# Two dense stages of a three-part kernel re-tiled from superblocks of 768 tokens to superblocks of 1024 and one of 512

## The chip, the cores and the metric

The kernel runs on one core of a Trainium2 chip. The metric is the time of one execution on the device in microseconds (us). Before the change it was 1660.44 us, the median of three runs (1659.65 to 1664.32).

## The reference

Attention within chunks of 64 tokens (8 batches, 8 heads, 576 tokens, head size 64), then two dense layers on the 4608 tokens that come out, in float32:

```python
scores = scale * q_c @ k_c.T                    # within chunks of 64
out = softmax(scores) @ v_c                     # -> x, 4608 x 512
h = x @ w_in                                    # first layer, 512 -> 2048
g = np.where(h > 0.0, h, np.exp(np.minimum(h, 0.0)) - 1.0)
x = g @ w_out                                   # second layer, 2048 -> 512
gate = 1.0 / (1.0 + np.exp(-(x @ w_gate)))      # 512 -> 1536
val = x @ w_val                                 # 512 -> 1536
return gate * val @ w_out2                      # last product, 1536 -> 512
```

## The kernel before

Every operand of a dense product is split into a high and a low part of type float32r, and each product of two operands is three matmuls (high by high, low by high, high by low: `PASSES`). From the second layer on, the matrices are also multiplied in seven products of half-size blocks in place of eight (Strassen's way, in Winograd's form): sums and differences of blocks are formed on VectorE, split, multiplied, and the seven results added up from the four pairs of PSUM banks `bank_x`, `bank_w`, `bank_y`, `bank_z` in the order `PRODUCTS`.

There are four stages, one after the other on TensorE.

- **First layer with attention** (`stage_1`, L367): blocks of 512 tokens, matmuls of 512 columns at L393. Its result goes to DRAM as `gd`, in nine blocks. At its end `one` finishes the last block.
- **Second layer** (`stage_2`, L668): superblocks of 2 x `NL` = 768 tokens, so six of them, matmuls of `NL` = 384 columns at L710. For each superblock there are seven products `i` with four parts `p` (`QM`), 12 matmuls per part. Beside each part, `beside` puts the work for the parts to come: `load_b` fetches raw blocks from `gd`, `sub_b` forms block differences, `split_b` splits for product `i + 1`. `after` adds a product up and stores to `ymid`.
- **Gate and value** (`unit`, L840): the same superblocks. `load_x`, `sum_x`, `split_x` prepare the seven inputs `xc` of a superblock; then six units `q` (`QU`), of seven products with 12 matmuls each at L849, in the order `seq`, which runs forwards and backwards by turns. Each unit evicts into two tiles `s` and `t`, takes sigmoids on ScalarE, and a `finish`, called in the next unit, multiplies gate by value on VectorE and stores to `gvd`.
- **Last product** (`product` in `stages_3_4`, L982): nine groups of 512 tokens, seven products of 36 matmuls of 256 columns.

All order is written out by hand: an engine does its instructions in program order, and a tile's slot is waited for where its last reader is not done. Two pools matter. The pool `w` has `NW` = 28 slots of 4 KB. It holds weights, the tiles of the weight conversion that goes on in the background (`convert_pairs`, stepped by `bg`), and small tiles by `four`. The pools `six_right` and `six_left` have 10 and 4 slots of 6 KB, handed out by `get` in the order in which they were freed; they hold raw blocks, splits (`gc`, `xc`), and `s` and `t`.

Weights come from DRAM in tiles of 512 KB (`wd`), issued on POOL's queue at L335. `hold(at, room, ahead)` looks at the list of all uses from position `at` on, drops what is used no more, and loads the next `ahead` different ones, as far as they have been converted; when more than `room` are held, the one whose next use is farthest goes. `room(...)` is 28 less its arguments. In the second layer `ahead` is 10, in gate and value 14, in its last three units 22:

```python
need = list(soon)[:min(ahead, room)]
...
while len(held) >= room:
    del held[max(held, key=soon.get)]
```

Loads of raw blocks and all stores of results go through SP's queue.

Of the kernel before, what the change touches and what calls it, by code (L numbers as in the profile page):

```python
# [36 lines left out]
EARLY = 2  # L37
SLACK = 4
# [8 lines left out]
NL = 384  # L47
NJ = NT // (2 * NL)
ML = NL // 128
# [9 lines left out]
def kernel(  # L59
# [14 lines left out]
    ymid = [dram.tile([128, 2, 2, 2, NL], F32, name=f"ymid{j}") for j in range(NJ)]  # L74
    gvd = [dram.tile([128, 4, QU, NL], F32, name=f"gv{j}") for j in range(NJ)]
# [263 lines left out]
    six, idle, owner = {}, [], {}  # L339

    def open_sixes(side, n):
        six[side] = ctx.enter_context(tc.tile_pool(name=f"six_{side}", bufs=n, side=side, reuse_waits="tile"))
        idle.extend([side] * n)
# [8 lines left out]
    right_first = []  # L352

    def get(key, shape, dtype=F32):
        p = idle.pop(idle.index("right") if right_first and "right" in idle else 0)
# [8 lines left out]
    def four(*shape):  # L364
        return shaped(w_p.tile([128, 1024], F32, tag="w", name="four"), shape)
# [275 lines left out]
    def load_x(j, h):  # L641
        t = xt[j, h] = get("x", (2, 2, NL))
        for k in range(2):
            nc.sync.dma_start(out=t[:, k], in_=ymid[j][:, h, k])

    def sum_x(j, i):
        lo, hi = xt[j, 0], xt[j, 1]
        if i == 1:
            t = xt[j, 2] = get("x", (2, 2, NL))
            nc.vector.tensor_sub(out=t[:, 0], in0=hi[:, 0], in1=lo[:, 0])  # L650
        elif i == 2:
            t = xt[j, 2]
            nc.vector.tensor_sub(out=t[:, 1], in0=hi[:, 1], in1=t[:, 0])
        elif i == 3:
            nc.vector.tensor_sub(out=hi[:, 0], in0=hi[:, 1], in1=hi[:, 0])
        elif i == 4:
            nc.vector.tensor_sub(out=lo[:, 1], in0=lo[:, 1], in1=xt[j, 2][:, 1])

    def split_x(j, i):
        n, k = ((0, 0), (2, 1), (2, 0), (1, 0), (0, 1), (1, 1), (0, 1))[i]  # L660
        t = xc[j, i] = get("xc", (2, 2, NL), F32R)
        split(xt[j, n][:, k], t[:, 0], t[:, 1], nc.scalar, nc.vector)
# [5 lines left out]
    def stage_2(one):  # L668
# [5 lines left out]
        def load_b(j, k):  # L674
            if j >= NJ:
                return
            par, h = KEYS[k]
            for s in range(2):
                t = raw[j, k, s] = get(k, (HF // 2, NL))
                at, end, o = (2 * j + h) * NL, (2 * j + h + 1) * NL, 0  # L680
                while at < end:
                    blk, c = divmod(at, TB)
                    n = min(TB - c, end - at)
                    nc.sync.dma_start(
                        out=t[:, :, o:o + n], in_=gd[blk][:, par, 4 * s:4 * s + 4, c:c + n],
                    )
                    at, o = at + n, o + n

        def sub_b(j, out, a, b, s):
            if j >= NJ:  # L690
                return
            if (j, out, s) not in raw:
                raw[j, out, s] = get(out, (HF // 2, NL))
            nc.vector.tensor_sub(out=raw[j, out, s], in0=raw[j, a, s], in1=raw[j, b, s])

        def split_b(j, i, p):
            if j >= NJ:
                return
            src = raw[j, FROM[i], p // 2][:, 2 * (p % 2):2 * (p % 2) + 2]
            t = gc[j, i, p] = get("gc", (2, 2, NL), F32R)  # L700
            split(src, t[:, 0], t[:, 1], nc.scalar, nc.vector)
            if i in (2, 3, 5, 6) and p % 2 == 1:
                free(raw.pop((j, FROM[i], p // 2)))

        def product(j, i, p):
            t, w = gc.pop((j, i, p)), held["mid", p, i]
            for k in range(2):
                for u in range(2):
                    for n, (zw, zx) in enumerate(PASSES):
                        nc.tensor.matmul(  # L710
                            out=bank[PRODUCTS[i]][:, u, 0:NL],
                            lhsT=w[:, k, zw, 128 * u:128 * u + 128],
                            rhs=t[:, zx, k],
# [4 lines left out]
            free(t)  # L718

        def after(j, i):  # L720
            ps = bank[PRODUCTS[i]][:, :, 0:NL]

            def new(k):
                three[k] = three_p.tile([128, 2, NL], F32, tag="three", name=k)
                return three[k]
# [23 lines left out]
        def beside(j, i, p):  # L749

            nxt, h, odd = j + 1, p // 2, p % 2 == 1
# [49 lines left out]
        open_sixes("right", 10)  # L801
        end = NB * HF
        for n in range(HF):
# [7 lines left out]
            hold(0, room(F1 - 2 * n - 2), SLACK + 1 + n)  # L811
        for j in range(NJ):
            for i in range(7):
                for p in range(QM):
                    product(j, i, p)
                    if j == i == p == 0:
                        one(end, False)
                        pa.close()
                        right_first.append(True)
                        open_sixes("left", 4)  # L820
# [3 lines left out]
                    beside(j, i, p)  # L824
                    if j == NJ - 1:
                        for f in first_x.get((i, p), ()):
                            f()
                    if (j, i, p) == (1, 0, 0):
                        hold(7 * QM, room(8), 10)
                        convert_pairs(range(PAIRS_1, PAIRS_2), nc.gpsimd)  # L830
                    if i in (2, 3, 5) and p > 0 and j > 0:
# [8 lines left out]
    def unit(n):  # L840
        j, q = seq[n]
        last, third = n % QU == QU - 1, n % QU == QU - 3
        for i, c in enumerate(PRODUCTS):
            ps = bank[c][:, :, 0:NL]
            w = held["glu", q, i]
            for b in range(2):
                for k in range(2):
                    for p, (zw, zx) in enumerate(PASSES):
# [3 lines left out]
                            rhs=xc[j, i][:, zx, k],  # L852
# [4 lines left out]
            if last:  # L857
                free(xc.pop((j, i)))
            hold(MID + 7 * n + i + 1, room(9 if todo else 0), 14 if n < len(seq) - 3 else 22)
            if i == 0:  # L860
                s, t = get("s", (2, 2, NL)), get("t", (2, 2, NL))
# [39 lines left out]
        def finish():  # L901
            nc.vector.tensor_tensor(out=s[:, :, 0], in0=s[:, :, 1], in1=s[:, :, 0], op=ALU.mult)
            nc.sync.dma_start(out=gvd[j][:, 0:2, q], in_=s[:, :, 0])
            nc.vector.tensor_tensor(out=c12[:, 0], in0=c12[:, 1], in1=c12[:, 0], op=ALU.mult)
# [5 lines left out]
    def stages_3_4():  # L910

        G = NT // 512
# [3 lines left out]
        def load_g(g, c):  # L916
            if g >= G:
                return
            t = cs[g, c] = get(c, (QU, 256))
            for k in range(2):  # L920
                j, m = divmod(2 * g + k, ML)
                nc.sync.dma_start(
                    out=t[:, :, 128 * k:128 * k + 128], in_=gvd[j][:, C[c], :, 128 * m:128 * m + 128],
                )
        def split_g(g, i, c, keep=False):
            src = cs[g, c] if keep else cs.pop((g, c))
            gc[g, i] = []
            for h in range(2):
                t = get("gc", (2, QU // 2, 256), F32R)
                split(src[:, 3 * h:3 * h + 3], t[:, 0], t[:, 1], nc.scalar, nc.vector)  # L930
                gc[g, i].append(t)
# [41 lines left out]
        def product(g, i):  # L973
# [4 lines left out]
            for q in range(QU):  # L978
                t, w = tiles[q // 3], held["out2", q // 2, i]
                for p, (zw, zx) in enumerate(PASSES):  # L980
                    for m in range(2):
                        nc.tensor.matmul(  # L982
                            out=po[c][:, m],
                            lhsT=t[:, zx, q % 3, 128 * m:128 * m + 128],
# [5 lines left out]
            for t in tiles:  # L990
                free(t)

        def after(g, i):
# [6 lines left out]
            def store(h):  # L1000
                for n in range(2):
                    j, m = divmod(2 * g + n, ML)
                    r = (2 * j + h) * NL + 128 * m
# [29 lines left out]
        for n in range(N):  # L1033
            if n == 2:
                hold(MID + 7 * n, room(9), 14)
# [74 lines left out]
```

## Time and profile before

| | |
|---|---|
| median of three runs | 1660.44 us |
| profiled execution | 1665.95 us |
| its span | 1664.2 us |
| TensorE busy | 1630.8 us (98%), 11484 matmuls |
| VectorE busy | 1204.4 us (72%) |
| ScalarE busy | 742.9 us (45%) |
| GpSimd busy | 248.9 us (15%) |
| DMA | 387.76 MB, mean 233 GB/s |

The span runs from the first to the last instruction of the profiled execution. Busy times are sums over the whole span; the stages differ, so they are read stage by stage. Matmuls are pipelined: the duration shown for a single one is longer than the distance from one to the next, so the price of a matmul is taken from the length of a run of them. In the rows PE is TensorE, PEld its weight loads, DVE is VectorE, ACT is ScalarE, POOL is GpSimd and SP is the engine that issues most loads and stores; L710 is line 710 of the kernel.

### The profile page before, as it was taken

To read this page: it belongs to the slowest core of one execution; us is meant where nothing else is said; L and a number is where in the kernel's file an instruction comes from. 1 tells how busy PE (TensorE), PEld (TensorE's weight loads), DVE (VectorE), ACT (ScalarE), POOL (GpSimd) and SP (SyncE) were. 2 spreads that over 40 slices of the span, in tenths; PEclk is the share of its full clock that TensorE was granted. 3 is DMA by queue.
4 is the path that set the end of the run, shared out by engine and by line. 5 is a ranking of instruction groups with operands and counts; after the bars stand their busy time and mean duration, and the time that the engine had idled before them with its cause. 6 is when DMAs were issued, how large, how long until landed. Compare 5 with 4: busy or idle time off the path is not lost.

```text
span 1664.2 us, 28660 instructions
## 1 busy us (share of the span) xinstructions
PE 1630.8 (98%) x11484; PEld 1526.8 (92%) x11484; DVE 1204.4 (72%) x1653; ACT 742.9 (45%) x1184; POOL 248.9 (15%) x413
## 2 busy tenths in 40 slices
PE   6899999999999999999999999999999999999998
PEld 4677777777789999999999999999999999999998
DVE  7778888888636799876865677765555647777776
ACT  5666667667544454434432433322221313334343
POOL 3332111222210021100121021313010120000000
PEclk9999999999999999999999999999999999999999
DMA  6668888899897589944788397787472696463641
GB/s 225 196 213 292 293 294 280 285 294 295 283 353 262 203 287 305 313 152 149 253 252 288 108 315 267 266 310 276 173 247 82 204 354 189 138 167 112 167 128 51
DMA packets 231445, 387.76 MB, mean 233 GB/s; under 512 B 14352, under 2 KB 134160, under 8 KB 230288
## 3 DMA queue, kind: packets, MB, share of 16 engines
q1 hardware_dynamic: 169344, 203.46, 37.8%
q0 software_dynamic: 61968, 182.48, 33.0%
q8 instruction: 90, 1.47, 0.4%
q14 instruction: 43, 0.35, 0.1%
HBM read 253.23 MB, written 132.64 MB: 232 GB/s over the span
## 4 chain that ended last, share of the span: by engine, by line
PE 80%; DVE 9%; ACT 6%; DMA 2%; issue 2%; POOL 0%; SPq 0%; ACTq 0%; DVEq 0%; POOLq 0%
PE bank_y L849 8%; PE bank_z L849 8%; PE bank_x L849 8%; PE bank_y L710 6%; PE bank_z L710 6%; PE bank_x L710 6%; PE bank_y L393 5%; PE bank_z L982 5%; PE bank_x L982 5%; PE bank_y L982 5%; PE bank_w L849 4%; PE bank_w L393 4%; PE bank_z L393 4%; PE bank_w L710 3%; PE bank_w L982 2%
## 5 line engine op out<-in xcount | busy, mean ns | idle before, releaser
L93 ACT CAST gc<-b 128x768 fp32r<-128x768 f32 x144 | 117.5, 834 | 117.4 <-PE bank_y L710 36.1
L849 PE MATMUL bank_y<-xc,w 128*128 128x384 f32 x864 | 163.6, 339 | 4.1 <-DVE s L102 4.1
L99 DVE TENSOR_TENSOR gc<-b,gc 128x768 fp32r<-128x768 f32 x144 | 134.1, 953 | 45.3 <-ACT gc L93 45.2
L849 PE MATMUL bank_z<-xc,w 128*128 128x384 f32 x864 | 161.9, 336 | 0.0
L849 PE MATMUL bank_x<-xc,w 128*128 128x384 f32 x864 | 161.4, 336 | 0.0
L849 PEld LDWEIGHTS bank_y<-xc,w 128*128 128x128 f32 x864 | 152.4, 190 | 5.2 <-DVE s L102 5.1
L865 ACT ACTIVATE s<-s 128x384 f32<-128x384 f32 x72 | 37.9, 526 | 266.2 <-DVE s L102 266.2
L849 PEld LDWEIGHTS bank_z<-xc,w 128*128 128x128 f32 x864 | 151.3, 188 | 0.0
L849 PEld LDWEIGHTS bank_x<-xc,w 128*128 128x128 f32 x864 | 150.7, 188 | 0.0
L393 PE MATMUL bank_y<-xs,w 128*128 128x512 f32 x576 | 140.6, 399 | 1.4 <-POOL w L165 0.9
L393 PE MATMUL bank_w<-xs,w 128*128 128x512 f32 x576 | 140.8, 399 | 0.0
L393 PE MATMUL bank_z<-xs,w 128*128 128x512 f32 x576 | 139.8, 398 | 0.0
L335 POOL DMA_DIRECT2D w<-wd_glu x139 | 74.4, 538 | 400.5 <-PE bank_x L849 137.8
L393 PEld LDWEIGHTS bank_y<-xs,w 128*128 128x128 f32 x576 | 107.7, 191 | 24.1 <-POOL w L165 1.2
L393 PEld LDWEIGHTS bank_z<-xs,w 128*128 128x128 f32 x576 | 107.8, 190 | 22.5
L393 PEld LDWEIGHTS bank_w<-xs,w 128*128 128x128 f32 x576 | 107.1, 190 | 22.2
L710 PE MATMUL bank_y<-gc,w 128*128 128x384 f32 x576 | 102.1, 336 | 0.0
L710 PE MATMUL bank_z<-gc,w 128*128 128x384 f32 x576 | 102.1, 336 | 0.0
L710 PE MATMUL bank_x<-gc,w 128*128 128x384 f32 x576 | 102.0, 336 | 0.0
L710 PEld LDWEIGHTS bank_x<-gc,w 128*128 128x128 f32 x576 | 100.3, 188 | 0.1
L710 PEld LDWEIGHTS bank_y<-gc,w 128*128 128x128 f32 x576 | 100.3, 188 | 0.0
L710 PEld LDWEIGHTS bank_z<-gc,w 128*128 128x128 f32 x576 | 100.3, 188 | 0.0
(145 smaller groups left out, 2942.3 us busy)
## 6 DMA issues: line engine op xcount, KB each, us to landing
w<-wd_glu POOLq DMA_DIRECT2D x139, 512.0 KB, 7.2
gd<-elu SPq DMA_DIRECT2D x72, 512.0 KB, 4.0
w<-wd_mid POOLq DMA_DIRECT2D x57, 512.0 KB, 7.9
c<-gv SPq DMA_DIRECT2D x72, 384.0 KB, 4.9
wd_glu<-ch POOLq DMA_DIRECT2D x36, 512.0 KB, 5.0
b<-gd SPq DMA_DIRECT2D x24, 768.0 KB, 6.6
raw<-in_qkv SPq DMA_DIRECT2D x61, 256.0 KB, 3.9
gv<-s SPq DMA_DIRECT2D x36, 384.0 KB, 5.0
```

Source lines behind the costliest of these rows:

```text
L93: nc.scalar.copy(out=out, in_=raw)
L99: lo_eng.tensor_sub(out=lo, in0=raw, in1=hi)
L335: nc.gpsimd.dma_start(out=t, in_=wd[m][q][:, (RIGHT if m == "out2" else LEFT)[i]])
L393: nc.tensor.matmul(out=h_bank(d)[:, n], lhsT=w[:, zw, kk * 128:(kk + 1) * 128], rhs=xs[j, kk][:, zx], start=(kk == 0 and p == 0), stop=(kk ...
L710: nc.tensor.matmul(out=bank[PRODUCTS[i]][:, u, 0:NL], lhsT=w[:, k, zw, 128 * u:128 * u + 128], rhs=t[:, zx, k], start=(i < 4 and p == 0 an ...
L849: nc.tensor.matmul(out=ps[:, b], lhsT=w[:, b, zw, 128 * k:128 * k + 128], rhs=xc[j, i][:, zx, k], start=(i < 4 and k == 0 and p == 0), sto ...
L865: nc.scalar.activation(out=x, in_=x if of is None else of, func=ACTF.Sigmoid)
L982: nc.tensor.matmul(out=po[c][:, m], lhsT=t[:, zx, q % 3, 128 * m:128 * m + 128], rhs=w[:, q % 2, zw], start=(i < 4 and q == 0 and p == 0 a ...
```

## The change

Superblocks become four of 1024 tokens and one of 512: `NLS` holds half their sizes, `START` where they begin. The second layer takes them in the order `ORDER`, the small one fourth; gate and value take them in their natural order, the small one last. Matmuls there have 512 columns, and 256 in the small superblock.

The slots of `get` become 8 KB (6 on the right, 4 on the left), and a rule that preferred slots on the right for a while goes. The splits of the second layer move to the pool `w`, two tiles of 4 KB in place of one of 6 KB; so do the last four of the seven inputs `xc` (from `XC` = 3 on), and a third of each split of the last product. So `hold` gets 8 slots less for weights: its calls name 8 more as taken. After the conversion's second part begins, `ahead` is 11 at first. A raw block of the second layer now lies within one block of `gd` and is one transfer, and so is each load of the last product. In one unit of each superblock the two multiplications of `finish` go to GpSimd.

```diff
-NL = 384
-NJ = NT // (2 * NL)
+NLS = (512, 512, 512, 512, 256)
+NJ = len(NLS)
+START = tuple(2 * sum(NLS[:j]) for j in range(NJ))
+ORDER = (0, 1, 2, 4, 3)
...
-        t = six[p].tile([128, 1536], dtype, tag="six", name=key)
+        t = slots[p].tile([128, 2048], dtype, tag="slot", name=key)
...
     def split_x(j, i):
-        t = xc[j, i] = get("xc", (2, 2, NL), F32R)
-        split(xt[j, n][:, k], t[:, 0], t[:, 1], nc.scalar, nc.vector)
+        x = xt[j, n][:, k]
+        if i < XC:
+            t = xc[j, i] = get("xc", (2, 2, NLS[j]), F32R)
+            split(x, t[:, 0], t[:, 1], nc.scalar, nc.vector)
+        else:
+            xc[j, i] = [four(2, NLS[j], dtype=F32R) for k in range(2)]
+            for k, t in enumerate(xc[j, i]):
+                split(x[:, k], t[:, 0], t[:, 1], nc.scalar, nc.vector)
...
         def split_b(j, i, p):
-            src = raw[j, FROM[i], p // 2][:, 2 * (p % 2):2 * (p % 2) + 2]
-            t = gc[j, i, p] = get("gc", (2, 2, NL), F32R)
-            split(src, t[:, 0], t[:, 1], nc.scalar, nc.vector)
+            for k in range(2):
+                t = gc[j, i, 2 * p + k] = four(2, NLS[j], dtype=F32R)
+                split(raw[j, FROM[i], p // 2][:, 2 * (p % 2) + k], t[:, 0], t[:, 1], nc.scalar, nc.vector)
...
-        open_sixes("right", 10)
+        open_slots("right", 6)
...
-                    hold((7 * j + i) * QM + p + 1, room(8 if todo else 0), 10)
-                right_first.clear()
+                    last = nxt is None and i >= 4
+                    hold((7 * o + i) * QM + p + 1, room(8, 8 if todo or last else 0), 10)
...
-            hold(MID + 7 * n + i + 1, room(9 if todo else 0), 14 if n < len(seq) - 3 else 22)
+                drop_x(j, i)
+            parts = 8 if n + 1 < len(seq) else 2 * (7 - max(i, XC - 1))
+            hold(MID + 7 * n + i + 1, room(parts, 9 if todo else 0), 14 if n < len(seq) - 3 else 22)
...
         def finish():
-            nc.vector.tensor_tensor(out=s[:, :, 0], in0=s[:, :, 1], in1=s[:, :, 0], op=ALU.mult)
+            eng = nc.gpsimd if n % QU == QU - 2 else nc.vector
+            eng.tensor_tensor(out=s[:, :, 0], in0=s[:, :, 1], in1=s[:, :, 0], op=ALU.mult)
...
-            for k in range(2):
-                j, m = divmod(2 * g + k, ML)
-                nc.sync.dma_start(
-                    out=t[:, :, 128 * k:128 * k + 128], in_=gvd[j][:, C[c], :, 128 * m:128 * m + 128],
-                )
+            nc.sync.dma_start(out=t, in_=gvd[j][:, C[c], :, 256 * k:256 * k + 256])
         def split_g(g, i, c, keep=False):
-                t = get("gc", (2, QU // 2, 256), F32R)
-                split(src[:, 3 * h:3 * h + 3], t[:, 0], t[:, 1], nc.scalar, nc.vector)
+            gc[g, i] = get("gc", (2, 4, 256), F32R), four(2, 2, 256, dtype=F32R)
+            for t, q in zip(gc[g, i], (slice(0, 4), slice(4, 6))):
+                split(src[:, q], t[:, 0], t[:, 1], nc.scalar, nc.vector)
...
-                hold(MID + 7 * n, room(9), 14)
+                hold(MID + 7 * n, room(8, 9), 11)
                 convert_pairs(range(PAIRS_2, len(tiles_of)), nc.sync)
```

## Rows read from the trace of the kernel before

**Rows 1.** Windows of 40 us: busy (instructions) by engine, clock, DMA share, GB/s.

```profile
560.00:600.00 40.00, 40.00 (x232) 40.00 (x231) 35.03 (x39) 19.05 (x28) 2.47 (x5) 1.00 0.59 194
...
640.00:680.00 40.00, 40.00 (x232) 40.00 (x232) 38.06 (x51) 23.30 (x34) 7.41 (x13) 1.00 0.89 288
...
880.00:920.00 40.00, 37.77 (x209) 37.45 (x208) 22.41 (x30) 9.52 (x17) 4.23 (x8) 0.96 0.76 265
...
1240.00:1280.00 40.00, 40.00 (x232) 40.00 (x231) 20.62 (x26) 7.91 (x14) 1.59 (x3) 1.00 0.40 147
```

**Rows 2.** Chain of waits in order of time, whole span: start us, us, what.

```profile
427.47 5.51 PE bank_y L393 x24
...
501.94 5.44 PE bank_z L393 x24
507.38 8.32 PE bank_x L710 x48
...
849.47 8.34 PE bank_z L710 x48
...
1403.86 4.28 PE bank_z L982 x36
```

**Rows 3.** Chain of waits from 857 to 925 us.

```profile
883.30 11.21 DMA craw<-in_w_out
...
899.72 3.77 PE bank_y L849 x12
903.50 2.08 PE bank_z L849 x12
...
922.27 2.10 PE bank_w L849 x12
```

**Rows 4.** Waits of TensorE: who for whom, total us, times, longest.

```profile
PE bank_y L849 <- DVE s L102: 4.1, 3, 2.2
```

**Rows 5.** Chain of waits from 940 to 1110 us.

```profile
1073.77 17.74 DMA gv<-t
...
1093.51 2.35 PE bank_y L849 x12
```

**Rows 6.** Groups by line and shape: busy us, mean ns, idle before, releasers.

```profile
L99 DVE TENSOR_TENSOR gc<-b,gc 128x768 fp32r<-128x768 f32 x144 | 134.1, 953 | 45.3 <-ACT gc L93 45.2
L93 ACT CAST gc<-b 128x768 fp32r<-128x768 f32 x144 | 117.5, 834 | 117.4 <-PE bank_y L710 36.1 <-PE bank_z L710 31.2 <-DVE gc L99 17.7
...
L694 DVE TENSOR_TENSOR b<-b,b 128x1536 f32<-128x1536 f32 x24 | 42.1, 1754 | 0.3
...
L287 DVE TENSOR_TENSOR ch<-cs,ch 128x512 fp32r<-128x512 f32 x52 | 35.2, 682 | 0.0
...
L416 DVE SCALAR_TENSOR_TENSOR elu<-bank_w,elu 128x1024 f32<-128x1024 f32 x24 | 29.3, 1219 | 12.8 <-ACT elu L411 12.8
...
L165 POOL TENSOR_TENSOR w<-t,w 128x512 fp32r<-128x512 f32 x16 | 23.5, 1493 | 11.8 <-ACT w L157 11.6
...
L287 DVE TENSOR_TENSOR ch<-ct,ch 128x256 fp32r<-128x256 f32 x26 | 10.9, 418 | 0.3 <-ACT ch L283 0.3
```

**Rows 7.** DMA issues of the page: KB each, median us to landing.

```profile
w<-wd_glu POOLq DMA_DIRECT2D x139, 512.0 KB, 7.2
...
w<-wd_mid POOLq DMA_DIRECT2D x57, 512.0 KB, 7.9
```

**Rows 8.** Instructions in order of time, POOL, 1296 to 1335 us.

```profile
1304.84 0.53 POOL L335 DMA_DIRECT2D w<-wd_glu  x1 [59.95 <-PE bank_x L849]
```

**Rows 9.** GB/s in 40 slices from 945 to 1120 us.

```profile
GB/s 33 0 0 228 196 135 351 395 395 410 395 398 412 400 395 411 404 396 27 149 37 0 0 180 184 138 336 395 398 409 391 395 381 392 400 414 415 279 150 46
```

**Rows 10.** Windows of chosen stretches, columns as in Rows 1.

```profile
1319.00:1376.00 57.00, 57.00 (x330) 57.00 (x329) 25.90 (x32) 10.96 (x19) 14.52 (x28) 1.00 1.07 347
...
1400.00:1410.00 10.00, 10.00 (x86) 10.00 (x86) 8.74 (x10) 4.20 (x6) 0.00 (x0) 1.00 1.15 285
1390.30:1659.83 269.53, 269.25 (x2268) 268.84 (x2268) 199.66 (x207) 105.43 (x144) 0.00 (x0) 1.00 0.46 131
```

More of the change, by code (lines that the diff above doesn't have):

```diff
@@ L37 @@
 EARLY = 2
+XC = 3
 SLACK = 4
@@ L73 @@
     gd = [dram.tile([128, 2, HF, TB], F32, name=f"gd{j}") for j in range(NB)]
-    ymid = [dram.tile([128, 2, 2, 2, NL], F32, name=f"ymid{j}") for j in range(NJ)]
-    gvd = [dram.tile([128, 4, QU, NL], F32, name=f"gv{j}") for j in range(NJ)]
+    ymid = [dram.tile([128, 2, 2, 2, n], F32, name=f"ymid{j}") for j, n in enumerate(NLS)]
+    gvd = [dram.tile([128, 4, QU, n], F32, name=f"gv{j}") for j, n in enumerate(NLS)]
     wd = {
@@ L337, in hold, with open_slots @@
             del held[max(held, key=soon.get)]
-    six, idle, owner = {}, [], {}
-    def open_sixes(side, n):
-        six[side] = ctx.enter_context(tc.tile_pool(name=f"six_{side}", bufs=n, side=side, reuse_waits="tile"))
+    slots, idle, owner = {}, [], {}
+    def open_slots(side, n):
+        slots[side] = ctx.enter_context(
+            tc.tile_pool(name=f"slots_{side}", bufs=n, side=side, reuse_waits="tile")
+        )
         idle.extend([side] * n)
@@ L350, in shaped @@
         return t[:, 0:n].rearrange(f"p ({names}) -> p {names}", **dict(zip("abc", shape)))
[L352 removed]
     def get(key, shape, dtype=F32):
[L355 to L356 removed]
+        p = idle.pop(0)
+        t = slots[p].tile([128, 2048], dtype, tag="slot", name=key)
         v = shaped(t, shape)
@@ L717, in product @@
                         )
-            free(t)
         def after(j, i):
-            ps = bank[PRODUCTS[i]][:, :, 0:NL]
+            ps = bank[PRODUCTS[i]][:, :, 0:NLS[j]]
             def new(k):
-                three[k] = three_p.tile([128, 2, NL], F32, tag="three", name=k)
+                three[k] = shaped(three_p.tile([128, 1024], F32, tag="three", name=k), (2, NLS[j]))
                 return three[k]
@@ L810, in stage_2 @@
                 sub_b(0, "b11", "b12", "b11", n - 6)
-            hold(0, room(F1 - 2 * n - 2), SLACK + 1 + n)
-        for j in range(NJ):
+            hold(0, room(F1 - 2 * n - 2, 8), SLACK + 1 + n)
+        for o, j in enumerate(ORDER):
+            nxt = ORDER[o + 1] if o + 1 < NJ else None
             for i in range(7):
@@ L910, in stages_3_4 @@
     def stages_3_4():
-        G = NT // 512
+        groups = [(j, k) for j in range(NJ) for k in range(NLS[j] // 256)]
+        G = len(groups)
         cs, gc, po, ut, ot = {}, {}, {}, {}, {}
@@ L978, in product @@
             for q in range(QU):
-                t, w = tiles[q // 3], held["out2", q // 2, i]
+                t, w = tiles[q // 4], held["out2", q // 2, i]
                 for p, (zw, zx) in enumerate(PASSES):
@@ L989, in product @@
                         )
-            for t in tiles:
-                free(t)
+            free(tiles[0])
         def after(g, i):
```

80 lines of the change are left out of this document (38 added, 42 removed).

## The prediction

> **What bounds the kernel now.** I read the 40 us windows first. TensorE is busy all 40 us in every window of the second layer, of gate and value and of the last product but for a few; the reader is to see 232 matmuls of 384 columns per 40 us, whatever VectorE does beside them (20.62 us in one window, 38.06 in another) [rows 1]. So in the two stages that the change touches, the end is set by how many matmuls there are and how long each takes; a faster neighbour is worth nothing there, a late one costs.
>
> The chain of waits, in order of time, gives the price of one matmul by its width [rows 2]. 512 columns: 24 in 5.44 us in the first layer, 226.7 ns. 384 columns: the second layer runs from 507.38 to 849.47 + 8.34 = 857.81, 350.4 us for 2016 matmuls, 173.8 ns. 256 columns: 36 in 4.28 us, 118.9 ns. Gate and value give 18.77 us for the nine products between 903.50 and 922.27, 108 matmuls, 173.8 ns again [rows 3]. At the full clock (2.4 GHz; the granted clock is 1.00 in these windows) the columns alone would take 213.3, 160.0 and 106.7 ns. What is left is 13.3, 13.8 and 12.2 ns: a cost per matmul that hardly depends on its width.
>
> Where TensorE does stand still is the start of gate and value: three waits, 4.1 us [rows 4]. The first stands at 883: a raw weight tile for conversion takes 11.21 us, ScalarE and VectorE queue behind it, and the product at 899.72 takes 3.77 us in place of 2.10, the window there showing a clock of 0.96 [rows 1, 3]. The last hangs on a gate-value store that took 17.74 us, whose slot the next superblock's input waits for; the product behind it takes 2.35 [rows 5]. With the slow products behind them these waits cost about 6 us.
>
> **The matmuls.** A product is 12 matmuls, 28 products per superblock in the second layer, 42 in gate and value. Before: 6 x 336 = 2016 and 6 x 504 = 3024, 5040 in all of 384 columns. After: 4 x 336 = 1344 and 4 x 504 = 2016 of 512, and 336 and 504 of 256. The columns stay equal (1,935,360); 840 matmuls go. Second layer: 1344 x 226.7 + 336 x 118.9 = 304.7 + 39.9 = 344.6 against 350.4, 5.8 us less. Gate and value: 457.0 + 59.9 = 516.9 against 3024 x 173.8 = 525.6, 8.7 us less. Together -14.5 us. The 512 price has two ends: 5.51 us per 24 where attention ran beside it (229.6 ns), which would give 3360 x 2.9 = 9.7 us back; and 5.44. I take 5.44, since the 384 rate is the same in busy and in quiet windows.
>
> The Trainium skill (TensorE: Matmul & The Clock Gate, Back-to-back issue gap) puts a warm isolated matmul at its columns over 2.4 GHz and about 2.5 ns. By that, 840 fewer matmuls are worth an estimated 2.1 us. The trace disagrees: 13 ns beyond the columns at all three widths.
>
> **Splits, second layer.** One 768-element split (ScalarE 834 ns, VectorE 953) becomes two of 512 (VectorE 682 each) [rows 6]. VectorE per large superblock: 56 x 0.682 = 38.2, eight raw sums of 2048 elements at 2.28 (from 953 at 768 and 1754 at 1536, 1.04 ns an element) = 18.3, five evictions of 1024 at 1.22 = 6.1; 62.6 us beside 336 x 0.2267 = 76.2 us of TensorE, 82%. Before: 28 x 0.953 + 8 x 1.754 + 5 x 0.953 = 45.5 beside 58.4, 78%. Conversions come to two superblocks both before and after, and the window with most of them, 95%, cost no stall [rows 1]. So nothing, hidden under the products. The tight place is the small superblock: 48 splits of 256 at 0.418, 8 of 512 for its successor, six sums of 1024 (1.22), two of 2048, five evictions of 512 make 40.8 us beside 39.9. Its last phase alone asks 5.5 + 4.6 + 0.7 = 10.8 us of VectorE in 5.7. But these splits are for the products of the next, 10.9 us long phase, which want them 2.7 us apart; walking through the order, each comes in time. Cost 0 to 5 us (that phase's excess), taken as 0.
>
> **Weight pool and loads.** Eight of the 28 weight slots now hold splits, so weights keep 20 where they kept 28. Following the eviction rule of `hold` through the list of uses gives, for before, 57, 139 and 21 loads; the page has 57 and 139 for the first two [rows 7]. For after it gives 102, 172 and 22: 79 more loads, 41 MB. Their issue on POOL waits for slots, and nothing on TensorE is queued behind it while they land in time. In a large superblock a weight is used every 2.72 us, at most 193 GB/s. Free.
>
> In the small superblock of gate and value a weight is used every 12 x 118.9 = 1.43 us, 367 GB/s, and the first group of the last product goes on at that pace. Six units and that group are 63 uses, 89.9 us. About 20 weights lie there at the start; 43 loads of 0.524 MB, 22.5 MB, follow. POOL asks as soon as a slot is free: before, the stage ends at 1390.3 [rows 10], so its last unit but one starts two units of 14.6 us earlier, at 1361, and that unit's loads were issued from 1304.84 on, one per product [rows 8]. With 20 slots that is some 28 us ahead. So they go out from 3 us on, and the last must be moved by about 86. Beside them go six units' stores (3.1 MB), group 0's and three of group 1's loads (3.1 and 2.4): 31.1 MB in 83 us, 375 GB/s. The rows: about 400 GB/s held for 48 us [rows 9]; 347 over 57 us in the same stage, where POOL asked for only one weight per 2.08 us; 285 where narrow loads ran almost alone [rows 10]. That makes 78, 90 or 109 us: 0, 7 or 26 us late. I take 2 us, between the first two, as the loads of the last stage also get rows twice as long.
>
> The Trainium skill (DMA: Bandwidth & Descriptors, Where 436 GB/s comes from) says that HBM binds such transfers at about 358 GB/s per core; by that the estimate is 87 us, 4 late. The 400 held above is over it.
>
> In the small superblock of the second layer 16 weights and 8.4 MB of raw tiles go in 40 us, 420 GB/s; but the last 4.2 MB are wanted only a superblock later. Cost 0 to 3 us, taken as 0.
>
> **The rest.** One `finish` per superblock goes to POOL: 1024 and 512 elements, by the 1493 ns of 512 [rows 6] about 4.5 us. Behind it in POOL's queue stand weight loads for more than a unit later; hidden, and it relieves VectorE in its fullest unit. In the small superblock it stands ahead of the last nine loads, of which the first is used some 20 us later: nothing, or a share of the lateness above. The last product's splits go from two of 768 (1.91 us of VectorE) to one of 1024 and one of 512 (1.90): nothing. The raw loads and those of the last stage become one transfer each with longer rows, SP's order stays. Without `right_first` the first differences lie in slots that the first layer's inputs held; its last matmul is done at 507.38 [rows 2], before they are computed: nothing.
>
> The early stalls: the wait at 883 starts three products before the conversion's first step; with products of 2.72 us in place of 2.08 the load has 1.9 us more, and VectorE's slack grows alike; the 17.74 us store had seven products, 14.6 us, and would have 19.0. Both are about covered. The gain lies between 0 and 6 us.
>
> **Sum.** The profiled execution took 1665.95 us, 1664.2 of span and 1.75 around it, 5.5 above the median of the runs (1660.44): it may have met more of these stalls. So I take 4 of the 6 us off its own time, 1665.95 - 14.5 - 4 + 2 = 1649.5, and 2 us off the median: 1660.4 - 14.5 - 2 + 2 = 1645.9. Predicted 1646.
>
> **Rivals.** (1) The tail becomes bound by transfers: the first group of the last product waits for weights. Place: the last unit of gate and value and that group. At 285 GB/s it costs 26 us for my 2, 1670, slower; it decides from 298 GB/s down (31.1 MB in 104.4 us, which is 1665.4). Against it the 347 and 400. 0.09. (2) Late splits: VectorE's excess at the small superblock reaches TensorE, 5 us, with the 3 us of weights there: 1651 to 1654, still faster. For it, 102% on paper; against it, no stall at 95%. 0.13. (3) 512 columns at 229.6 ns: 1655.6, on the border. 0.08, halved between faster and same. (4) No cost per matmul is saved: the time goes by columns, 173.8 / 384 = 0.453 ns each, so 512 take 231.7 ns; 3360 of them and 840 of 256 are 878.4 against 876.0, 1662.8, within 0.3%. Against it stand the 226.7 ns; for it only that they come from another layer's operands. 0.06. The Trainium skill's 2.5 ns per matmul (TensorE: Matmul & The Clock Gate, Back-to-back issue gap) would by my estimate end on the same side, near 1658.
>
> **How the numbers follow.** My forecast, 1639 to 1651, has 0.64. Anything under 0.3% (5 us) is no change that a measurement here can tell. Faster 0.64 + 0.13 + 0.04 = 0.81; same 0.04 + 0.06 = 0.10; slower 0.09. The range goes from 1638 (all early stalls gone, no late weight) to 1657 (229.6 ns, or 7 us of late weights with late splits).
>
> **What would show it.** 24 matmuls of 512 in 5.44 us and 12 of 256 in 1.43 in both stages; the second layer in about 345 us; TensorE without idle at the small superblock; 102, 172 and 22 weight loads; no wait on a weight at the start of the last product. Wrong if 512-column products take 5.5 us or more per 24 beside the splits, or if TensorE waits for `w` or for a split around the two small superblocks.

## The result, and the profile after

The kernel with the change takes 1680.16 us (median of six runs, 1676.07 to 1681.07) against 1661.03 for the kernel before (six runs): a ratio of 1.0105 [1.0090, 1.0121]. It is slower, where the prediction said 1646 and gave slower a chance of 0.09. The profiled execution took 1680.64 us, 14.7 more than that of before. (The line numbers below are those of the kernel after: L721 is the second layer, L859 gate and value, L990 the last product, L934 the loads of the last product's blocks, L915 and L917 the stores of `s` and `t`.)

Where is it lost? First the windows, cut at the stages and at the small superblocks (profile of after; columns as in [rows 1]):

```profile
503.82:732.30 228.48, 228.48 (x1011) 189.25 (x1010) 193.53 (x250) 114.87 (x200) 46.01 (x83) 1.00 0.93 315
732.30:776.45 44.15, 40.99 (x338) 40.47 (x337) 32.95 (x64) 24.03 (x57) 7.93 (x15) 1.00 1.05 397
776.45:852.64 76.19, 76.19 (x337) 63.09 (x337) 66.31 (x80) 35.27 (x62) 14.27 (x27) 1.00 0.71 216
852.64:1315.76 463.12, 460.62 (x2018) 378.43 (x2018) 285.45 (x324) 133.12 (x210) 103.04 (x164) 1.00 0.77 263
1315.76:1398.89 83.13, 63.78 (x505) 63.17 (x504) 32.77 (x52) 14.82 (x34) 25.33 (x46) 0.90 1.04 357
1398.89:1674.53 275.64, 274.44 (x2268) 272.21 (x2268) 199.06 (x207) 105.00 (x144) 0.00 (x0) 0.99 0.39 128
```

The first number after the stretch is its length, the next TensorE's busy time. Wherever superblocks are large, the two are equal or nearly so. The second layer takes 348.8 us, 1.6 less than before. The small superblock of gate and value (fifth row) should take 504 x 118.9 ns = 59.9 us and takes 83.1, TensorE being busy for 63.8 of them, at a granted clock of 0.90 and with the DMA engines full. Gate and value come to 546.3 us (before 532.5), the last product to 275.6 (before, cut likewise, 269.5). The first stage, which the change does not touch, ended 3.6 us earlier here; over the profiles of the kernels below its end moves between 503.0 and 506.9.

The waits of TensorE (profile of after; who for whom, total us, times, longest) name the places. Before, there were the 4.1 us of [rows 4] in these stages and half a microsecond at the start of the last product:

```profile
PE bank_x L859 <- ACT s L878: 10.3, 1, 10.3
PE bank_x L859 <- DVE t L890: 7.1, 1, 7.1
...
PE bank_y L721 <- DMA w<-wd_mid: 2.6, 2, 2.3
PE bank_y L859 <- DVE s L104: 2.5, 1, 2.5
PE bank_x L990 <- ACT gc L95: 1.9, 1, 1.9
```

Three of them, 10.3, 7.1 and 1.9 us, lie in the small superblock of gate and value and at its end. TensorE's instructions in order of time (start, us, idle time before and what ended it) show what follows each:

```profile
1364.32 1.60 PE L859 MATMUL bank_z<-four,w 128*128 128x256 f32 x12
1373.03 2.93 PE L859 MATMUL bank_x<-xc,w 128*128 128x256 f32 x12 [7.11 <-DVE t L890]
1375.76 2.15 PE L859 MATMUL bank_w<-xc,w 128*128 128x256 f32 x12
...
1391.12 2.93 PE L859 MATMUL bank_x<-four,w 128*128 128x256 f32 x12 [10.34 <-ACT s L878]
```

The product behind a long wait takes 2.73 us from its start to the next one's, where others take 1.41 to 1.45: TensorE comes back at the lower of its two clock levels (granted clock 0.50 from 1373.00 to 1375.76, that is 1.2 GHz of 2.4). Waits 19.35, slow products 3.3: that is the 23.2 us, nearly.

None of these three waits is for a weight. ScalarE, in order of time, shows what the two long ones stood for:

```profile
1372.13 0.38 ACT L876 ACTIVATE t<-bank_x 128x256 f32<-128x256 f32 x1 [9.35 <-DMA gv<-s]
...
1390.48 0.59 ACT L878 COPY s<-bank_x 128x512 f32<-128x512 f32 x1 [15.66 <-DMA gv<-s]
```

ScalarE is to evict a bank into a tile `s` or `t`, and the tile's slot is held by an earlier unit's result whose store has not landed. SP's queue and the chain of waits (start, us, what) show why the stores are late:

```profile
1331.05 0.42 SPq L934 DMA_DIRECT2D c<-gv  x1
1340.11 0.36 SPq L915 DMA_DIRECT2D gv<-s  x1
...
1354.26 0.36 SPq L934 DMA_DIRECT2D c<-gv  x1
1354.71 0.50 SPq L915 DMA_DIRECT2D gv<-s  x1
...
1375.29 0.36 SPq L934 DMA_DIRECT2D c<-gv  x1
1375.75 0.49 SPq L915 DMA_DIRECT2D gv<-s  x1
```

```profile
1340.11 14.08 DMA gv<-s
...
1355.30 19.94 DMA gv<-t
...
1375.75 14.63 DMA gv<-s
```

A store goes out at 1340.11 and lands 14.08 us later. The load of a block for the last product (L934) wants that slot, so it waits until 1354.26, and the next stores stand behind it. Behind the load's 768 KB the next stores take longer still, the one of `t` 19.94 us; the next load waits for it. The store behind that load takes 14.63 us, and ScalarE's eviction at 1390.48 waits for its slot. The slots are fewer too: 10 of 8 KB where there were 14 of 6 KB. All of it happens at full DMA engines (1300 to 1400, GB/s in 40 slices, then issues with KB each and median us to landing):

```profile
GB/s 94 325 0 0 0 7 0 100 264 288 401 405 417 390 392 391 391 387 394 385 386 390 411 392 390 386 392 383 395 406 415 339 390 392 399 386 378 114 296 336
...
w<-wd_glu POOLq DMA_DIRECT2D x22, 512.0 KB, 10.7
w<-wd_out POOLq DMA_DIRECT2D x22, 512.0 KB, 11.6
c<-gv SPq DMA_DIRECT2D x4, 768.0 KB, 15.5
gv<-s SPq DMA_DIRECT2D x5, 256.0 KB, 14.6
```

From 1325 to 1392 it holds some 390 GB/s. The Trainium skill (DMA: Bandwidth & Descriptors, Where 436 GB/s comes from) puts the HBM limit of such transfers at about 358 GB/s per core, which is half of what it gives for a stack with two cores. Here one core runs, the trace shows more, as in [rows 9], and the measured 390 decide.

### The profile page after: what moved, and what is told of

It is laid out like the page before. It is cut to its first block, busy times and chain, and to the rows that moved or that the text cites. A ratio compares the mean times of both kernels' runs of the same rounds, so it can differ in the third digit from the quotient of the medians.

```text
span 1678.9 us, 27430 instructions
## 1 busy us (share of the span) xinstructions
PE 1624.6 (97%) x10644; PEld 1385.7 (83%) x10644; DVE 1205.5 (72%) x1703; ACT 752.4 (45%) x1277; POOL 308.9 (18%) x502
## 4 chain that ended last, share of the span: by engine, by line
PE 72%; DVE 12%; ACT 6%; DMA 6%; issue 2%; SPq 1%; POOL 0%; ACTq 0%; DVEq 0%; POOLq 0%
PE bank_x L859 8%; PE bank_y L859 8%; PE bank_z L859 8%; PE bank_y L721 6%; PE bank_z L721 6%; PE bank_x L721 6%; PE bank_x L990 5%; PE bank_z L990 4%; PE bank_w L859 4%; PE bank_y L395 4%; PE bank_w L395 3%; PE bank_z L395 3%; PE bank_w L721 3%; PE bank_y L990 3%; PE bank_w L990 2%
## 5 line engine op out<-in xcount | busy, mean ns | idle before, releaser
L95 ACT CAST four<-b 128x512 fp32r<-128x512 f32 (+1 forms) x240 | 129.1, 576 | 81.4 <-PE bank_y L721 30.9
L101 DVE TENSOR_TENSOR four<-b,four 128x512 fp32r<-128x512 f32 (+1 forms) x240 | 141.3, 632 | 33.3 <-ACT four L95 32.5
L859 PE MATMUL bank_z<-four,w 128*128 128x512 f32 (+1 forms) x720 | 158.5, 369 | 0.0
L859 PEld LDWEIGHTS bank_z<-four,w 128*128 128x128 f32 x720 | 126.3, 189 | 23.4
L721 PE MATMUL bank_y<-four,w 128*128 128x512 f32 (+1 forms) x480 | 100.7, 368 | 3.2 <-DMA w<-wd_mid 2.6
L337 POOL DMA_DIRECT2D w<-wd_mid x102 | 54.4, 537 | 267.1 <-DVE four L101 58.2
L721 PE MATMUL bank_x<-four,w 128*128 128x512 f32 (+1 forms) x480 | 100.2, 368 | 0.0
L721 PE MATMUL bank_z<-four,w 128*128 128x512 f32 (+1 forms) x480 | 100.2, 368 | 0.0
L721 PEld LDWEIGHTS bank_y<-four,w 128*128 128x128 f32 x480 | 83.8, 188 | 18.6 <-issue 2.5
L721 PEld LDWEIGHTS bank_x<-four,w 128*128 128x128 f32 x480 | 83.8, 189 | 15.0
L721 PEld LDWEIGHTS bank_z<-four,w 128*128 128x128 f32 x480 | 83.8, 189 | 14.9
L104 DVE TENSOR_TENSOR s<-bank_z,s 128x1024 f32<-128x1024 f32 (+1 forms) x60 | 66.9, 1115 | 37.6 <-PE bank_z L859 37.2
L859 PE MATMUL bank_x<-four,w 128*128 128x512 f32 (+1 forms) x360 | 80.1, 373 | 10.3 <-ACT s L878 10.3
```

The costliest lines, as they stand in the source:

```text
L95: nc.scalar.copy(out=out, in_=raw)
L101: lo_eng.tensor_sub(out=lo, in0=raw, in1=hi)
L104: nc.vector.tensor_tensor(out=out, in0=a, in1=b, op=ALU.add)
L337: nc.gpsimd.dma_start(out=t, in_=wd[m][q][:, (RIGHT if m == "out2" else LEFT)[i]])
L721: nc.tensor.matmul(out=bank[PRODUCTS[i]][:, u, 0:NLS[j]], lhsT=w[:, k, zw, 128 * u:128 * u + 128], rhs=t[:, zx], start=(i < 4 and p == 0 a ...
L859: nc.tensor.matmul(out=ps[:, b], lhsT=w[:, b, zw, 128 * k:128 * k + 128], rhs=x_part(j, i, zx, k), start=(i < 4 and k == 0 and p == 0), st ...
```

## The experiments

The expectations speak of theories: A, the amount of traffic in the small last superblock; B, the order of SP's queue, loads of the last product ahead of the stores; C, the last product's fourth split, which is late in every group. Ratios are to the kernel before.

**The small superblock elsewhere.**

```diff
-NLS = (512, 512, 512, 512, 256)
-ORDER = (0, 1, 2, 4, 3)
+NLS = (512, 512, 512, 256, 512)
+ORDER = (0, 1, 2, 3, 4)
```

> The small superblock comes fourth in gate and value too, a large one is last. Theory A (the last small superblock and the first group of the last product ask together for weights at 367 GB/s, transfers fill up at some 390, the stores of s and t take 14 to 20 us, their slots are not free, evictions and then TensorE wait): behind the short units there are now products of 2.72 us instead of the last product's new weights, so the overload is shorter; the 19 us of waits shrink to under 8, the time comes to about 1662 to 1668 us. Theory B (SP's order: the loads c of group 0 wait for a slot and the stores stand behind them): those loads no longer meet the short units, the waits go altogether, about 1657 us.

1672.6 us, 1.0066 [1.0052, 1.0080]: 7.6 less than the change, a smaller gain than either theory gave. The long waits are gone, but in the small superblock there are three waits for VectorE's `s` (6.7 us) and four for a weight (3.0 us) instead, and it takes 73.6 us (1203.01 to 1276.61). So it cost at both places tried in gate and value.

**Same place, fewer loads.** All units of the small superblock use the weights of unit 0, so that 35 of its products load nothing.

```diff
-    uses += [("glu", q, i) for _, q in seq for i in range(7)]
+    uses += [("glu", 0 if j == NJ - 1 else q, i) for j, q in seq for i in range(7)]
...
-            w = held["glu", q, i]
+            w = held["glu", 0 if j == NJ - 1 else q, i]
```

> The units of the last, small superblock all use the weights of unit 0, so 35 products there reload nothing; this leaves out the right weights of that superblock, and its part of the output differs. Slots, stores and loads of c stay. Theory A: without the weights' 18 MB the stores land in about 5 us, no wait in the small superblock, which takes 60 us in place of 83; 1655 to 1660 us in all. Theory B: SP's order and the ten slots are the same, at least half of the waits stays, 1668 us or more.

1660.25 us, 0.9992 [0.9983, 1.0001]: 20 less than the change. With SP's order as it was, the small superblock and the end of the large ones cost what the matmuls do:

```profile
1316.00:1379.30 63.30, 62.06 (x513) 61.54 (x511) 34.34 (x54) 16.03 (x37) 7.85 (x13) 1.00 0.53 172
```

(The nine matmuls above 504 are of the last large unit; the small superblock itself runs from 1317.70.) Its stores land in 2.2 us (`s`) and 2.7 us (`t`, medians), where those of the change take 14.6 and 15.9. So without the traffic the stalls are gone, but for 1.3 us at the start of the last product: neither the order nor the ten slots do harm by themselves.

**SP's order.** The first three loads of the last product are asked for two to four units earlier.

```diff
-            (N - 4, 0): lambda: load_g(0, "c12"),
-            (N - 3, 0): lambda: load_g(0, "c22"),
-            (N - 2, 0): lambda: load_g(0, "c11"),
+            (N - 6, 0): lambda: [load_g(0, c) for c in ("c12", "c22", "c11")],
```

> The loads of c12, c22 and c11 for group 0 are issued at the first product of the small superblock, into the three slots just free, before the transfers fill up; after that SP has only the stores of s and t until c21. Theory A: the stores are still slow beside the weights and only four slots are left for s and t, so TensorE waits as long as now or longer, 1678 to 1690 us. Theory B: the stores no longer stand behind a load that waits, the waits go, 1657 to 1662 us.

1671.43 us, 1.0057 [1.0042, 1.0073]: 8.7 less than the change, with the same weights loaded at the same rate. The issues between 1300 and 1400 us in this run:

```profile
w<-wd_glu POOLq DMA_DIRECT2D x22, 512.0 KB, 6.6
...
gv<-s SPq DMA_DIRECT2D x6, 256.0 KB, 7.0
gv<-t SPq DMA_DIRECT2D x6, 256.0 KB, 8.9
```

The stores land in 7.0 and 8.9 us instead of 14.6 and 15.9. Two waits are left. 3.2 us hang on a store of the last large unit that takes 13.16 us, right behind the three loads that were moved; 5.0 us, at the start of the last product, on its first split, whose slot comes free with a store of `t` that takes 9.61 us. The time lies between the numbers of the two theories, and it takes both: full engines make each transfer slow, and the queue's order strings the slow ones behind each other.

**The last product's splits.** The chain of the kernel after at the start of a group's fourth product:

```profile
1440.32 0.69 DVE four L104
1441.01 1.68 DVE c L960
...
1442.76 1.06 ACT gc L95
...
1443.84 1.24 DVE gc L101
...
1445.12 0.98 PE bank_z L990 x6
```

An eviction, a difference and the two steps of the split's first tile take 4.67 us one after the other, where the third product gives 4.28. TensorE begins the fourth with the high parts and stops for the low ones. In order of time the 24 matmuls that read that tile take longer than those of the product before:

```profile
1440.12 2.99 PE L990 MATMUL bank_y<-w,gc 128*128 128x256 f32 x24
...
1444.38 3.37 PE L990 MATMUL bank_z<-w,gc 128*128 128x256 f32 x24
```

That is 0.38 us, taken for each of nine groups. With the third in the pool `w` first, the first tile has two of six column blocks, not four:

```diff
-            gc[g, i] = get("gc", (2, 4, 256), F32R), four(2, 2, 256, dtype=F32R)
-            for t, q in zip(gc[g, i], (slice(0, 4), slice(4, 6))):
+            gc[g, i] = four(2, 2, 256, dtype=F32R), get("gc", (2, 4, 256), F32R)
+            for t, q in zip(gc[g, i], (slice(0, 2), slice(2, 6))):
```

> The last product's splits do the third in the weight pool first and the two thirds in the 8 KB slot second. Theory C (in each group the fourth product waits some 0.45 us, because VectorE's eviction, difference and a first split of 1024 elements take 4.8 us of a product's 4.28): the first part is ready about 0.9 us earlier, the wait in all nine groups goes, 4 us less than with the change, about 1676 us. Rival: the wait comes from the difference alone, nothing changes, 1680 us.

1676.81 us, 1.0088 [1.0074, 1.0102]: 3.4 less, and 9 x 0.38 = 3.4. In the profile the last product takes 272.3 us in place of 275.6, so theory C holds at its size.

**No superblock of 256 columns.** Three superblocks of 1024 and two of 768, in natural order; loads that cross a block of `gd` go in pieces.

```diff
-NLS = (512, 512, 512, 512, 256)
-ORDER = (0, 1, 2, 4, 3)
+NLS = (512, 512, 512, 384, 384)
+ORDER = (0, 1, 2, 3, 4)
```

> Superblocks of three times 1024 and twice 768 tokens: five as with the change, the same 4200 matmuls in the two stages, none narrower than 384 columns; raw blocks that cross a block border and one load group come in two pieces again. Refined theory (the cost of the change sits in the small superblock, where a weight per 1.43 us fills the transfers to some 390 GB/s, in both stages, and the rest of the matmul gain is real): no wait on w in the second layer, no wait before the last product beyond 1 us; second layer about 345 us, gate and value 521 to 525, the last product 4 us longer than before as with the change; 1652 to 1657 us. Rival (the new pools, with 20 slots for weights and ten large slots, cost it): waits of about 20 us remain, 1670 us or more.

1656.63 us, 0.9971 [0.9961, 0.9981]: faster than before. It saves 840 matmuls like the change; by their prices they are worth 12.7 us here (2520 of 512 columns, 1680 of 384) and 14.5 there. From the second layer on TensorE waits 2.9 us at the start of gate and value and little else. With the third first as well:

> As two_of_384, with the third in the weight pool split first in the last product. Refined theory: the waits of the last product go too, 1648 to 1653 us, faster than the kernel before by 8 to 13 us. Rival: 1667 us or more.

1653.64 us, 0.9950 [0.9931, 0.9970], 0.6 us above what was expected.

**The new pools alone.** All six superblocks 768 tokens again, but slots and splits as in the change (`NLS` six times 384):

> Six superblocks of 768 tokens as before the change, in the new pools: 8 KB slots, splits in the weight pool, 20 slots for weights, one finish per superblock on GpSimd. No wide products and no small superblock. Refined theory: the pools alone cost the 4 us in the last product's splits and nothing else, 1662 to 1667 us. Rival (the pools cost it): 1675 us or more.

1679.29 us, 1.0109 [1.0091, 1.0128], some 15 us above what was expected and where the rival put it: as slow as the change, without any small superblock. Is it the slots taken from the weights, or the rest? In the kernel before, with only the calls of `hold` changed so that eight slots fewer hold weights:

```diff
-                    hold((7 * j + i) * QM + p + 1, room(8 if todo else 0), 10)
+                    hold((7 * j + i) * QM + p + 1, room(8, 8 if todo or (j == NJ - 1 and i >= 4) else 0), 10)
...
-            hold(MID + 7 * n + i + 1, room(9 if todo else 0), 14 if n < len(seq) - 3 else 22)
+            parts = 8 if n + 1 < len(seq) else 2 * (7 - max(i, 2))
+            hold(MID + 7 * n + i + 1, room(parts, 9 if todo else 0), 14 if n < len(seq) - 3 else 22)
```

> The kernel before, with only the numbers in the calls of hold as the change has them: 8 slots less for weights, which then lie idle or serve as buffers. If what the new pools cost at 384 columns (18 us in all_384, of which the last product has some 5) comes from the weights that are loaded again, this shows most of the rest: 1668 to 1674 us, about 300 loads of weights. If it comes from the splits or from the ten large slots, the time stays at 1661 to 1664 us.

1679.98 us, 1.0104 [1.0087, 1.0121]: 18 us for eight slots, with the shorter `ahead` of 11 that goes with them, and nothing else; more than expected. Its waits and issues (profile of this run):

```profile
PE bank_x L849 <- DVE t L880: 5.9, 1, 5.9
...
PE bank_y L849 <- DVE s L102: 3.8, 3, 2.1
PE bank_w L710 <- ACT gc L93: 2.4, 3, 1.4
```

```profile
w<-wd_glu POOLq DMA_DIRECT2D x194, 512.0 KB, 9.6
w<-wd_mid POOLq DMA_DIRECT2D x113, 512.0 KB, 12.5
```

In [rows 7] these were 139 and 57 loads, landing in 7.2 and 7.9 us. By the chain of waits the second layer runs from 505.57 to 864.90, 8.9 us more than before, and gate and value to about 1405.7, 8.3 more. As in the kernel after, the waits are not for `w`: they are for splits and evictions behind other transfers. The raw blocks of 768 KB land in 11.4 us (median) where they took 6.6, and the chain of waits names a raw block and a store:

```profile
607.56 25.21 DMA b<-gd
...
1037.49 11.20 DMA gv<-t
```

All waits in gate and value lie before 1153 us, while the background conversion runs (its last store goes out at 1152.1) and takes slots of the pool `w` too. From 1153 to 1405.7, with 20 slots for weights and no conversion, TensorE is busy for 252.5 of 252.7 us. In the version with two superblocks of 768 these come last, in gate and value from 1200.5 us on, where the conversion ends at 1209.4, and show no wait either. So in gate and value the price is that of the slots with the conversion beside it, not of 384 columns by themselves.

**Asking earlier in the second layer.** The small superblock there loses 3.9 us, waiting for `w` at 767.44 (the load took 16.13 us at 396 GB/s). With `hold` asking 14 ahead instead of 10:

```diff
-                    hold((7 * o + i) * QM + p + 1, room(8, 8 if todo or last else 0), 10)
+                    hold((7 * o + i) * QM + p + 1, room(8, 8 if todo or last else 0), 14)
```

> As with the change, but the second layer asks for weights 14 uses ahead, not 10. If the wait of TensorE on w in the small superblock there (2.6 to 4.2 us with the slow restart) comes from a lead of 14.3 us against a landing of up to 16 us, 20 us of lead end it: 3 to 4 us less, 1676 us. If the transfers are simply full there, it stays, 1680 us.

1680.15 us, 1.0113 [1.0096, 1.0130]: no change. The wait is gone and the second layer takes 345.0 us, 3.8 less; gate and value take 549.3, 3.0 more. But single profiles of the same code vary by as much there: up to the last product's first split the version with the third first is the kernel after, and it took 351.1 and 541.6 us where that took 348.8 and 546.3. Why the gain does not show in the whole time is not settled.

**The early stall.** In the kernel after, TensorE still waits at 907 (chain of waits):

```profile
880.87 0.77 SPq L646
...
884.81 16.28 DMA craw<-in_w_out
...
907.18 3.02 PE bank_y L859 x12
```

A raw tile for conversion takes 16.28 us (11.21 in [rows 3]): the loads of the next inputs (L646), a third larger than before, stand just ahead of it in SP's queue. In the version with two superblocks of 768 and the third first, the conversion makes no step in that unit:

```diff
-            if not last and not third:
+            if not last and not third and n != 2:
```

> As two_of_384_third (1653.6 us), but the background conversion does no step in unit 2 of gate and value, so its first step comes in unit 4, some 38 us later; loads and their order stay. Theory (the raw tiles for conversion stand in SP's queue behind the next superblock's inputs, land after 16.9 us, and ScalarE and VectorE queue behind the first step): the wait of 3.2 us with its slow restart goes, 4 to 6 us less, 1648 to 1650 us. Rival (the wait is VectorE's load in that unit): unchanged, 1653 us.

1646.65 us, 0.9903 [0.9884, 0.9921], the best version: 7.0 less by the medians, a little more than expected. Its second layer and its gate and value (windows, as above):

```profile
504.00:849.00 345.00, 345.00 (x1682) 305.76 (x1681) 292.71 (x393) 173.73 (x319) 67.84 (x124) 1.00 0.91 305
849.00:1369.31 520.31, 520.28 (x2522) 458.64 (x2521) 317.01 (x375) 147.39 (x244) 129.33 (x211) 1.00 0.84 287
```

TensorE has no idle time left there. How much of it is the same line in the kernel before?

> The kernel before, with no conversion step in unit 2 of gate and value. If the count of matmuls is what late_steps (1646.7 us) gains, this loses only the first wait and its slow restart, some 4 us: 1657 us, 10 us above late_steps (12.7 by the prices of the matmuls for three 1024 and two 768 superblocks, less 2 for the first products of a unit). If late_steps owes its time to the moved steps, this comes to 1650 us or less.

1657.4 us, 0.9980 [0.9970, 0.9989], as expected: 3.3 of the 15 us that the best version gains. Between the two versions lie 10.75 us by the medians and 12.8 by the ratios, each to the kernel before on its own chip; by their prices the 840 matmuls are worth 12.7. In the two profiles TensorE waits nowhere in these stages, and there the second layer takes 345.0 against 350.4 us, gate and value 520.3 against 526.1: 11.2 us together.

**The change, mended.** Its own sizes, with the third first, the early loads, 14 ahead and no step in that unit:

> The sizes of the change, with the third split first, the loads c of group 0 early, weights 14 uses ahead in the second layer and no conversion step in unit 2. If the parts add up: 1680 less 3.4, 8.7, 0 to 4 and 7, about 1658 us, no longer slower than the kernel before, but 11 us behind late_steps, for the small superblock of gate and value still fills the transfers. If the small superblock is harmless once nothing stands in SP's queue, 1648 us.

1660.46 us, 0.9996 [0.9986, 1.0006]. Waits of 4.1 us in the small superblock of gate and value and of 1.4 and 2.6 us behind it are left; it stands 13.8 us behind the version with two superblocks of 768.

**Two looks at what is left.** `finish` wholly on VectorE again (`eng = nc.vector`), and the order in which a product accumulates (loops over `k` and `b` exchanged), both in the version with two of 768 and the third first:

> As two_of_384_third, with all multiplications of finish on VectorE as before the change. I expect no difference, 1652 to 1655 us, as VectorE has slack in gate and value. Rival: VectorE in the last unit of a superblock comes late, 2 us or more slower.

1653.46 us, 0.9942 [0.9925, 0.9959]: nothing, as expected, though its profile has a wait of 2.2 us for a split at the start of the last product.

> As two_of_384_third, with the loops over k and b in gate and value exchanged, so that the two halves of a bank take turns as in the second layer. If the order of the accumulation costs the 0.03 us by which the first four products of a unit exceed 2.72 us at 512 columns, they come to 2.72; otherwise they stay at 2.75 to 2.77.

1654.08 us in one run: nothing. It was meant for the chain of a large unit of gate and value (kernel after):

```profile
1304.83 2.77 PE bank_z L859 x12
1307.60 2.72 PE bank_x L859 x12
```

The first three or four products of a unit take 2.75 to 2.77 us, the others 2.72, and they did so with either order. The cause stays open.

## Why the prediction was wrong

**Right.** The price of a matmul: in the chain of after, 48 of 512 columns take 10.88 us in each part of the second layer's large superblocks (226.7 ns), 48 of 256 take 5.76 (120.0):

```profile
656.14 10.88 PE bank_x L721 x48
...
738.06 5.76 PE bank_w L721 x48
```

The loads: the page of after counts

```profile
w<-wd_glu POOLq DMA_DIRECT2D x172, 512.0 KB, 8.6
w<-wd_mid POOLq DMA_DIRECT2D x102, 512.0 KB, 6.9
```

and 22 for the last product, the three numbers predicted. The saving per matmul is real (11 to 13 us where 12.7 were worked out, in the version with two superblocks of 768). VectorE hides the second layer's splits but for one wait of 0.5 us in the small superblock, and `finish` on GpSimd is worth nothing in that version. Rival 4 is dead, and rival 2's late splits came with half a microsecond in place of 5.

**The step that failed** is "Weight pool and loads". It priced 79 more loads as free beside large superblocks and as 2 us at the end of gate and value, where the small superblock cost 23.2. Its weights were nearly exact (43 loads foreseen, 44 issued), and its rate held: 390 GB/s where 375 were needed. That its whole, 31.1 MB, meets the 31.02 MB moved between 1300 and 1400 is in part chance: the stores of the last two large units are in the second number, and group 1's loads came later. But it asked only whether the weights would land in time, and at the end of gate and value they did. It did not ask what full engines do to everybody else: a store of 256 KB needs 14 to 20 us, where those of 512 KB issued by 1322, before the engines are full, land in 4.7 and 6.3 (median), its slot comes free late, a load waits for that slot in SP's queue, and the next stores wait behind the load. Rival 1 had the place and the cause, full engines, with the wrong victim, and it was to decide from 298 GB/s down, where the engines held 390. The part itself speaks of the loads of group 0 and 1 as bytes; as instructions in SP's queue they were not followed. Of the prediction's own signs of being wrong two appeared, small: 2.6 us of waits for `w` in the second layer's small superblock, and 1.9 us for a split at the start of the last product.

The 79 more loads come from the eight lost slots, and that such a loss can cost was shown in the kernel before: 18 us, with the conversion beside it. The large superblocks hide it (their one wait, the early stall, was there before the change), and so do two of 768 behind the conversion. That a weight is used there only every 2.72 or 2.08 us, against 1.43 in the small one, is the likely reason; it was not tested by itself. That is the change's one real trade, and a superblock of 256 columns is where it did not pay.

**Terms of another size.** The small superblock of the second layer: taken as 0 of 0 to 3, measured 3.9, for the weight that the part did name. "The last product's splits ... nothing": the sum of VectorE's work was right (1.90 us), but the split's first tile grew from three column blocks to four and is on the path of each group's fourth product; 3.4 us. "The early stalls ... both about covered", 2 to 4 us of gain: only the second went; the raw load took 5.1 us longer than before, behind input loads that had grown (their order in the queue is seen; that their size is the cause was not tested). The 7 us were to be had (last step of the best version) by moving the conversion, not by wider products. The gate and value matmuls at 226.7: the first products of a unit lie 0.03 to 0.05 us above, about 0.15 per unit, 3.6 in all with the slow product behind the early stall, not foreseen and not explained.

**Adding up,** from the predicted 1645.9: 21.2 at the end of gate and value, 3.9 in the second layer, 3.6 for first products, 6.1 in the last product (splits 3.4; its first product takes 6.9 us, before 5.0), and the 2 us of early stalls, taken as not gained at all, make 1682.7; 1680.2 was measured. The terms are read from one profile, and 2.5 us are within what two profiles of the same code differ by.

That a version of this change takes 1646.65 is no support for the forecast: it has other sizes, and two repairs that the prediction did not have.

## What to carry to other kernels

When a change adds transfers to a stretch that nearly fills the DMA engines, price not only the arrival of what is added but each other transfer there at its loaded duration, and follow whose slot it holds and what stands behind it in its queue. Buffer slots that cache weights are bandwidth: count the loads per us of compute before and after in the narrowest stage, not in the mean one. A rest of another width pays the whole cost of the narrow shape; here two middling sizes beat a large one with a remainder.

## What the runs showed of the hardware

A 256 KB store of `s` took 14.6 us (median of five) in the kernel after, where 768 KB loads stand among the stores in SP's queue, and 7.0 (median of six) where three of these loads were asked for earlier, both with the engines at about 390 to 400 GB/s; where the weights of that stretch were left out, at a mean of 172 GB/s, it took 2.2. Weight loads on POOL's queue, which are twice that size, landed in 10.7 and 6.6 us in the same two runs. After an idle stretch of 7 us TensorE's next product took twice its time (2.73 us against 1.42, at a granted clock of 0.50), and after those of under half a microsecond in the last product it did not.
